# Weight decoding: more rooms for raw words, one operation moved to GpSimd and one to VectorE, a later subtraction

## The chip, the cores and the metric

The kernel runs on one core of a Trainium2 chip. A core has a matrix engine (TensorE, PE in the profile; its weight loads are PEld), three engines for elementwise work (VectorE, DVE; ScalarE, ACT; GpSimd, POOL) and SyncE (SP), whose queue issues nearly all DMA transfers here. Every engine runs its own list of instructions in order and waits on semaphores for the others. The metric is the time of one execution on the device, in microseconds (us); less is better.

## The reference

Attention with a band and a few global keys, followed by a dense MLP. There are 4 batches of 8 heads, 768 positions, head size 64; each position attends to the 8 global keys and to the 96 positions up to its own, with a linear bias by distance. The heads side by side give 3072 rows of 512, which the MLP takes through weights 512x2048 and 2048x512.

```python
def _attn_ref(q, k, v, n_global, n_local):
    scores = scale * np.matmul(q, k.transpose(0, 1, 3, 2))
    ...
    scores = np.where(keep, scores + bias, -1e9)
    a = np.exp(scores - np.max(scores, axis=-1, keepdims=True))
    return np.matmul(a / (a.sum(-1, keepdims=True) + 1e-9), v)

def _moe_ref(x, w_in, w_out):
    h = x @ w_in
    g = h * np.clip(h + 3.0, 0.0, 6.0) / 6.0
    return g @ w_out
```

q, k, v are fp32; the weights are float64, so the kernel gets each of them as two 32-bit words.

## The kernel before

The 3072 rows are 8 blocks of 384 (a batch and half of its positions). For each block four pairs of heads are attended to, and then the MLP runs over 16 columns of 128 of the hidden width. One such step f is a group of 12 matmuls (`first`, L166: four slices of 128 of the input, and three products each, high x high, low x high, high x low, since every fp32 value is split into a rounded high part and the rest), a gate (ScalarE L177, VectorE L178), the gate's own split into `gh` (a rounded copy) and `gl` (L191, VectorE), and 9 matmuls (`second`, L198). The second group waits for `gl`.

**Stages.** First the attention of blocks 0 to 2, 12 pairs, runs as a pipeline written out in `banded` (L529 to L576): scores on TensorE, weighing on VectorE (L831), exponentials on ScalarE (L835), division by the row sums on GpSimd (`normalize`, L855), transposes back on TensorE (`turn`, L863 and L865), and the product with the values (L907). From pair 10 on, the first steps of block 0's MLP are woven in. Then the rest of block 0 runs together with block 1, alternating, so that every weight is used twice. During all of this the weights are decoded. Blocks 2 to 7 follow with their weights ready, and with the attention of the block behind them woven in.

**Decoding.** There are 32 chunks of weights (128x512 values, 512 KB of raw words each; chunk 2f holds step f's part of the first weights, chunk 2f+1 that of the second). A chunk's tile `wst` comes by DMA (`fetch`, L363). The rest turns each float64 into fp32 with integer operations on its words:

- L371 ScalarE: absolute value of the high word (into `wz`)
- L378 GpSimd (the first 12 chunks, `helped`) or L400 VectorE (the other 20): clamp of the exponent
- L401 VectorE: mask and shift left by 3
- L409 VectorE: merge with sign and top bits of the high word
- L375 GpSimd: the low word times 2^-29, rounded (`we`)
- L415 VectorE: integer add of `we` to `wz`
- L419 ScalarE: the high part (`w1h`, `w2h`), a rounded copy
- L406 VectorE: the low part (`w1l`, `w2l`), by subtraction, one chunk later

`wst`, `wz` and `we` have two buffers each. The fetch of chunk i+2 comes after the merge of chunk i, which is the last to read that chunk's `wst`.

**What sets the order.** `decode` is a generator with four steps per chunk. `work(pe, dve)` keeps two sums, the TensorE time handed out and the VectorE time handed out, and lets out decoding steps as long as VectorE's sum is behind; each `yield` says what a step counts as. `decoded_to` forces steps out before the matmuls that need a chunk. `in_order` (L613) then fixes the order of TensorE, SyncE and GpSimd as the code issued it; for VectorE and ScalarE a scheduler picks the order at build time, the earlier issued first where both could run. So on GpSimd a division stands behind whatever decoding operation was let out before it. `held` is the last instruction of the first pairs' weighing; decoding's first instruction is tied behind it.

`general` is a fallback for other sizes of the band; it does not run here.

Of the kernel before, what the change touches and what calls it, by code (L numbers as in the profile page):

```python
# [9 lines left out]
F32 = mybir.dt.float32  # L10
F32R = mybir.dt.float32r
I32 = mybir.dt.int32
U32 = mybir.dt.uint32
AF = mybir.ActivationFunctionType
ALU = mybir.AluOpType
# [3 lines left out]
DM, DF = 512, 2048  # L19
P = 128  # L20
# [5 lines left out]
NF = DF // P  # L26
# [12 lines left out]
LEAST, MOST = (float(np.uint32(e << 20).view(np.float32)) for e in (896, 1151))  # L39
# [8 lines left out]
LEAD = 6  # L48
WAKE = 9
FIRST = 6  # L50

def store(nc, pool, out, row, acc, last=False):
    for tt in range(NT):
        o = pool.tile([P, DM], F32, name="o")
        nc.scalar.mul(out=o, in_=acc[tt], mul=1.0 / 6.0)
        (nc.scalar if last and tt == NT - 1 else nc.sync).dma_start(out=out[row + tt * P: row + (tt + 1) * P, :], in_=o)


class Kernel:
# [15 lines left out]
    def decoding(self, ctx, loads, bufs, **kw):  # L75

        self.wp = self.pool("wp", loads, ctx=ctx, **kw)
        self.zp = self.pool("zp", bufs, ctx=ctx, **kw)
        self.ep = self.pool("ep", bufs, ctx=ctx, **kw)

    def weights(self):

# [279 lines left out]
        self.raw[i] = self.wp.tile([P, 2 * DM], I32, name="wst")  # L362
        self.nc.sync.dma_start(out=self.raw[i], in_=self.w[i])  # L363

    def magnitude(self, i):


        words = self.raw[i].rearrange("p (c w) -> p c w", w=2)
        self.z[i] = self.zp.tile([P, DM], I32, name="wz")
        self.e[i] = self.ep.tile([P, DM], I32, name="we")  # L370
        self.nc.scalar.activation(out=self.z[i].bitcast(F32), in_=words[:, :, 1].bitcast(F32), func=AF.Abs)  # L371
        if i == 0:
            self.tc.add_manual_dep(self.nc.cur_bb.bb.instructions[-1], self.held, mybir.DependencyInfo(
                mybir.DependencyClass.NoSync, mybir.DependencyReason.DATA), reason="behind the first pairs")
        self.nc.gpsimd.tensor_scalar(out=self.e[i], in0=words[:, :, 0].bitcast(U32), scalar1=2.0 ** -29, scalar2=0.0, op0=ALU.mult, op1=ALU.add)  # L375
        if self.helped(i):
            z = self.z[i].bitcast(F32)
            self.nc.gpsimd.tensor_scalar(out=z, in0=z, scalar1=MOST, scalar2=LEAST, op0=ALU.min, op1=ALU.max)  # L378

    def helped(self, i):  # L380
        return i < 2 * FIRST

    def part(self, i, w1, w2):
        f = i // 2
        return (self.w1(w1, f), lambda a: a.rearrange("p (k c) -> p k c", k=NKT)) if i % 2 == 0 else (self.w2(w2, f), lambda a: a)

    def decode(self):

        nc = self.nc
        ts, stt, tt = nc.vector.tensor_scalar, nc.vector.scalar_tensor_tensor, nc.vector.tensor_tensor
        N = 2 * NF
        self.magnitude(0)
        for i in range(N + 1):
            a, b = i < N, i > 0
            if a:
                z = self.z[i]
                if not self.helped(i):
                    ts(out=z.bitcast(F32), in0=z.bitcast(F32), scalar1=LEAST, scalar2=MOST, op0=ALU.max, op1=ALU.min)  # L400
                ts(out=z, in0=z, scalar1=0x07FFFFFF, scalar2=3, op0=ALU.bitwise_and, op1=ALU.logical_shift_left)  # L401
            yield (0.34 if self.helped(i) else 0.68) * a
            if b:
                hi, sh = self.part(i - 1, self.w1h, self.w2h)
                lo, _ = self.part(i - 1, self.w1l, self.w2l)
                tt(out=lo, in0=sh(self.z.pop(i - 1).bitcast(F32)), in1=hi.bitcast(F32), op=ALU.subtract)  # L406
            yield 0.6 * b
            if a:
                stt(out=z, in0=self.raw[i].rearrange("p (c w) -> p c w", w=2)[:, :, 1], scalar=-0x40000000, in1=z,  # L409
                    op0=ALU.bitwise_and, op1=ALU.bitwise_or)  # L410
                if i + 2 < N:
                    self.fetch(i + 2)
            yield 0.6 * a
            if a:
                tt(out=z, in0=z, in1=self.e.pop(i), op=ALU.add)  # L415
                if i + 1 < N:
                    self.magnitude(i + 1)
                hi, sh = self.part(i, self.w1h, self.w2h)
                nc.scalar.copy(out=hi, in_=sh(z.bitcast(F32)))  # L419
            yield 0.69 * a  # L420

    def work(self, pe, dve):

# [5 lines left out]
    def decode_step(self):  # L429
        self.given[1] += next(self.decoding_steps)  # L430
        self.decoded += 1
        if self.decoded == 4 * (2 * NF + 1):
            self.decoded_all()

    def decoded_to(self, i):

        while self.decoded < 4 * (i + 1) + (2 if i < 2 * NF - 1 else 4):
            self.decode_step()

    def halves(self, steps, pool=False):  # L440
# [45 lines left out]
    def banded(self, flag):  # L486
# [6 lines left out]
        self.ps_x = self.pool("ps_x", 1, PSUM)  # L493
        self.turn, self.more, self.score_banks = {}, True, 1
        self.wake()
        self.raw, self.z, self.e, self.given, self.decoded = {}, {}, {}, [0.0, 0.0], 0
        self.last, self.op = None, None
        self.weights()
        with ExitStack() as early, ExitStack() as words:
            x0 = self.x_tiles(self.pool("x0", 1, ctx=early, side="right"))  # L500
            xs = [x0, self.x_tiles(), self.x_tiles()]
            self.decoding(words, 2, 2, side="right")
            self.decoding_steps = self.decode()

            def decoded_all():
# [3 lines left out]
            self.decoded_all = decoded_all  # L509
            self.fetch(0)  # L510
            self.given[1] = LEAD
            self.allowed = 4 * NF + 3
            acc = []
            with ExitStack() as ctx:
                self.room += self.rooms(self.pool("more", 1, ctx=ctx), MORE - ROOMS, ROOMS)
# [1 line left out]
                self.fetch(1)  # L517
                for n in range(ROOMS):
                    self.load(n, True)
                self.plain_distances(ctx)  # L520
                self.attending(ctx, 0, 9, 5)
                pairs = [Pair(self, n, xs[n // NPAIR], True) for n in range(EARLY)]
                todo = self.halves([(0, f, xs[0], acc) for f in range(FIRST)])

# [52 lines left out]
                for _ in todo:  # L577
                    pass
            self.weights()
            self.allowed = 4 * (2 * NF + 1)  # L580
            acc1 = [pool.tile([P, BANK], F32, name=name) for pool, name in ((self.ps_s, "sp"), (self.ps_t, "tp"), (self.ps_x, "xp"))]
            self.given[1] = max(self.given)
            todo = [(1, f, xs[1], acc1) for f in range(FIRST)]
            todo += [(i, f, xs[i], (acc, acc1)[i]) for f in range(FIRST, NF) for i in range(2)]
            for _ in self.halves(todo):
# [65 lines left out]
    def general_setup(self):  # L651
        self.constants()
        self.ps_o = self.pool("ps_o", NT, PSUM)
        self.common(1, 2)
        self.weights()
        self.weights()
        self.decoding(self.ctx, 1, 1)
        self.ap_ = self.pool("ap", 1)
        self.dp = self.pool("dp", 1)
        self.up = self.pool("up", 1)  # L660
        self.mp = self.pool("mp", NT)
        self.op = self.pool("op", 1)
        nc = self.nc
        ts, tt = nc.vector.tensor_scalar, nc.vector.tensor_tensor
        iv = self.dp.tile([P, 4], I32, name="iv")
        nc.sync.dma_start(out=iv, in_=self.bounds.broadcast_to([P, 4]))
        fv = self.dp.tile([P, 2, 2], F32, name="fv")
        nc.vector.tensor_copy(out=fv.rearrange("p a b -> p (a b)"), in_=iv)
        c = self.dp.tile([P, 2, 1], F32, name="c")
        lv = self.lv = self.dp.tile([P, 2, 1], F32, name="lv")  # L670
        ts(out=c, in0=fv[:, :, 0:1], scalar1=0.0, scalar2=None, op0=ALU.is_lt)
        tt(out=c, in0=c, in1=fv[:, :, 1:2], op=ALU.add)
        ts(out=c, in0=c, scalar1=2.0 ** 32, scalar2=None, op0=ALU.mult)
        tt(out=lv, in0=c, in1=fv[:, :, 0:1], op=ALU.add)
        self.masked = self.dp.tile([P, S], F32, name="masked")
        nc.vector.memset(self.masked, NEG)
# [84 lines left out]
class Pair:  # L761
# [61 lines left out]
    def weigh(self, t, sp, e, lo):  # L823
        nc, kk = self.nc, self.k
        for j in range(2):
            h, i = 2 * self.pr + j, 2 * t + j
            if self.plain:
                d, scale = (kk.p0 if lo else kk.p1)[:, h], PLAIN
            else:
                d, scale = (kk.d0 if lo else kk.d1), SLOPES[h]  # L830
            nc.vector.tensor_tensor_reduce(out=e[:, j, lo:W], in0=sp[j][:, lo:W], in1=d, op0=ALU.add, op1=ALU.min, scale=scale,  # L831
                                           scalar=3.0e38, accum_out=self.least[:, i:i + 1])
        for j in range(2):
            i = 2 * t + j
            nc.scalar.activation(out=e[:, j, lo:W], in_=e[:, j, lo:W], func=AF.Exp, bias=self.least[:, i:i + 1], scale=-1.0,  # L835
                                 accum_out=self.sums[:, 0, i:i + 1])
        if self.n <= 2:
            kk.held = nc.cur_bb.bb.instructions[-1].name
        self.rows.append(e)

    def sum_up(self, t=None):
# [145 lines left out]
```

## Time and profile before

| | us |
|---|---|
| median of 3 runs | 676.46 |
| lowest, highest | 675.81, 677.81 |
| span of the profiled execution, first to last instruction | 675.4 |
| TensorE busy in it | 658.0 |
| VectorE busy in it | 421.2 |
| GpSimd busy in it | 230.2 |

The profiled execution's own time is given as its span; the median of the timed runs is 1.1 us more, for what lies before the first and after the last instruction. The profile lists, for each engine, how long it was busy, and in slices or stretches of time in which share; for a group of instructions (one source line, one form) the count, the busy time and the mean duration, and what ended the idle time before them; and who waited for whom. In a list in order of time each line has the start, the duration, the engine, the source line, the operation, what it writes and reads, and in brackets how long the engine had been idle and what released it. Line numbers are those of the kernel before. Durations of operations that follow each other on one engine overlap a little.

### The profile page before, as it was taken

Reading aid. Unit: us, or ns where it says so; the run is one execution under the profiler, and the core shown is the slowest. Engines: PE = TensorE matmul, PEld = TensorE weight load, DVE = VectorE, ACT = ScalarE, POOL = GpSimd, SP = SyncE. Lnnn points to the kernel's source line nnn. Section 1 sums busy time; section 2 is a strip of 40 time slices with the busy share of each in tenths; the row PEclk is TensorE's granted clock in tenths of the full one; section 3 lists DMA queues with packets and bytes.
Section 4 is the critical chain, followed back from the end, with each engine's and each line's share of the span. In section 5 each row is a group of like instructions: output and inputs, shape, how many; then the busy total and the mean of one; then the engine's idle time right before and its main releaser. Section 6 shows DMA issues by size and latency. Waiting matters only on the chain.

```text
span 675.4 us, 11454 instructions
## 1 busy us (share of the span) xinstructions
PE 658.0 (97%) x3963; PEld 587.2 (87%) x3963; DVE 421.2 (62%) x1109; ACT 278.5 (41%) x736; POOL 230.2 (34%) x401
## 2 busy tenths in 40 slices
PE   9989599999999999999999999999999999999997
PEld 7769488888999999989998999899898999989995
DVE  6798889999324776557663777547763677422222
ACT  6898555655225433143332444143331434221111
POOL 5778642221001443324341444314531444302110
PEclk9999889999999999999999999999999999999999
DMA  8675444442003267635654266734455255610001
GB/s 290 185 249 183 168 151 154 138 144 94 1 1 113 67 167 195 167 95 139 151 148 125 93 161 175 195 94 117 129 166 152 71 154 142 141 48 2 1 1 52
DMA packets 60836, 84.73 MB, mean 125 GB/s; under 512 B 8416, under 2 KB 45536, under 8 KB 60768
## 3 DMA queue, kind: packets, MB, share of 16 engines
q1 hardware_dynamic: 60480, 83.64, 42.7%
q8 instruction: 33, 0.54, 0.3%
q14 instruction: 35, 0.29, 0.1%
q10 hardware_dynamic: 288, 0.26, 0.1%
HBM read 62.92 MB, written 20.97 MB: 124 GB/s over the span
## 4 chain that ended last, share of the span: by engine, by line
PE 79%; DVE 9%; DMA 5%; ACT 3%; POOL 2%; issue 2%; SPq 0%; POOLq 0%; ACTq 0%; DVEq 0%
PE hp L166 34%; PE acc L198 32%; DMA wst<-w 5%; PE xp L907 2%; PE sp L820 2%; PE tp L907 2%; DVE wz L409 2%; PE tp L820 2%; ACT n L835 2%; DVE wz L415 1%; POOL n L855 1%; PE xp L358 1%; DVE wz L401 1%; DVE n L831 1%; DVE gl L191 1%
## 5 line engine op out<-in xcount | busy, mean ns | idle before, releaser
L177 ACT ACTIVATE g<-hp,small 128x384 f32<-128x384 f32 x127 | 73.7, 580 | 251.6 <-PE hp L166 230.5
L166 PE MATMUL hp<-xh,w1h 128*128 128x384 f32 x512 | 174.0, 340 | 0.0
L166 PE MATMUL hp<-xh,w1l 128*128 128x384 f32 x512 | 172.7, 337 | 0.0
L166 PE MATMUL hp<-xl,w1h 128*128 128x384 f32 x512 | 171.9, 336 | 0.0
L184 POOL TENSOR_SCALAR gh<-g 128x384 fp32r<-128x384 f32 x96 | 51.8, 540 | 292.3 <-DVE g L178 261.7
L198 PE MATMUL acc<-w2h,gl 128*128 128x512 f32 x336 | 133.8, 398 | 0.2
L198 PE MATMUL acc<-w2l,gh 128*128 128x512 f32 x336 | 133.1, 396 | 0.0
L198 PE MATMUL acc<-w2h,gh 128*128 128x512 f32 x336 | 132.9, 395 | 0.0
L178 DVE SCALAR_TENSOR_TENSOR g<-g,hp 128x384 f32<-128x384 f32 x128 | 69.7, 545 | 90.1 <-ACT g L177 89.7
L191 DVE TENSOR_TENSOR gl<-g,gh 128x384 fp32r<-128x384 f32 x128 | 80.6, 630 | 53.2 <-POOL gh L184 44.9
L855 POOL TENSOR_SCALAR n<-n,sums 128x232 f32<-128x232 f32 (+1 forms) x186 | 103.1, 570 | 31.2 <-DVE sums L846 17.6
L835 ACT ACTIVATE n<-n,least 128x232 f32<-128x232 f32 (+1 forms) x192 | 89.3, 468 | 44.0 <-DVE least L831 42.0
L166 PEld LDWEIGHTS hp<-xh,w1h 128*128 128x128 f32 x512 | 96.3, 188 | 5.5 <-issue 1.5
L166 PEld LDWEIGHTS hp<-xl,w1h 128*128 128x128 f32 x512 | 96.2, 188 | 3.9
L166 PEld LDWEIGHTS hp<-xh,w1l 128*128 128x128 f32 x512 | 96.0, 188 | 0.0
L198 PEld LDWEIGHTS acc<-w2h,gl 128*128 128x128 f32 x336 | 63.4, 189 | 15.4 <-DVE gl L191 1.7
L198 PEld LDWEIGHTS acc<-w2h,gh 128*128 128x128 f32 x336 | 63.8, 190 | 10.4 <-POOL gh L184 0.3
L198 PEld LDWEIGHTS acc<-w2l,gh 128*128 128x128 f32 x336 | 63.6, 189 | 10.4
L880 DVE STREAM_TRANSPOSE blocks<-n 128x256 f32<-128x256 f32 x112 | 43.5, 424 | 30.5 <-POOL n L855 17.3
L375 POOL TENSOR_SCALAR we<-wst 128x512 int32<-128x512 uint32 x32 | 26.6, 832 | 64.6 <-DMA wst<-w 56.7
L791 POOL TENSOR_SCALAR kx<-load 64x504 fp32r<-64x504 f32 (+1 forms) x40 | 31.1, 778 | 43.9 <-PE hp L166 42.3
L831 DVE CUSTOM_DVE_ANT_0 n<-sp,d 128x232 f32<-128x232 f32 (+1 forms) x70 | 23.6, 374 | 29.6 <-PE sp L820 29.1
(111 smaller groups left out, 788.3 us busy)
## 6 DMA issues: line engine op xcount, KB each, us to landing
wst<-w SPq DMA_DIRECT2D x32, 512.0 KB, 3.5
load<-pairs SPq DMA_DIRECT2D x22, 636.0 KB, 5.2
there<-blocks SPq DMA_DIRECT2D x52, 256.0 KB, 2.6
load<-pairs SPq DMA_DIRECT2D x32, 384.0 KB, 4.2
weights<-there SPq DMA_DIRECT2D x48, 192.0 KB, 3.9
out<-o SPq DMA_DIRECT2D x23, 256.0 KB, 2.1
weights<-there SPq DMA_DIRECT2D x32, 160.0 KB, 3.2
load<-pairs SPq DMA_DIRECT2D x9, 444.0 KB, 4.2
```

Of the source, the lines that this page charges most:

```text
L166: self.nc.tensor.matmul(hp, lhsT=self.w1(w, f)[:, kt, :], rhs=a[:, kt, :], start=(n == 0), stop=(n == 3 * NKT - 1))
L177: nc.scalar.activation(out=g, in_=hp, func=AF.Relu, bias=self.three, scale=1.0)
L178: nc.vector.scalar_tensor_tensor(out=g, in0=g, scalar=6.0, in1=hp, op0=ALU.min, op1=ALU.mult)
L184: self.nc.gpsimd.tensor_scalar(out=gh, in0=g, scalar1=1.0, scalar2=0.0, op0=ALU.mult, op1=ALU.add)
L191: self.nc.vector.tensor_tensor(out=gl, in0=g, in1=gh.bitcast(F32), op=ALU.subtract)
L198: self.nc.tensor.matmul(acc[tt], lhsT=a[:, tk], rhs=self.w2(w, f), start=(f == 0 and j == 0), stop=(f == NF - 1 and j == 2))
L791: nc.gpsimd.tensor_scalar(out=part["kx"][own, c], in0=k[own, c], scalar1=1.0, scalar2=0.0, op0=ALU.mult, op1=ALU.add)
L820: nc.tensor.matmul(sp[j][:, lo:W], lhsT=q[:, t], rhs=part["kx"][:, c], start=(m == 0), stop=(m == 1))
L831: nc.vector.tensor_tensor_reduce(out=e[:, j, lo:W], in0=sp[j][:, lo:W], in1=d, op0=ALU.add, op1=ALU.min, scale=scale, scalar=3.0e38, accum ...
L835: nc.scalar.activation(out=e[:, j, lo:W], in_=e[:, j, lo:W], func=AF.Exp, bias=self.least[:, i:i + 1], scale=-1.0, accum_out=self.sums[:, ...
L855: nc.gpsimd.tensor_scalar(out=e[:, j, lo:W], in0=e[:, j, lo:W], scalar1=over, scalar2=0.0, op0=ALU.mult, op1=ALU.add)
L880: nc.vector.transpose(out=blocks[:, :, s].rearrange("p b j q -> p j b q"), in_=e[:, :, c:c + P].rearrange("p j (b q) -> p j b q", b=4))
```

## The change

- `wst` gets four buffers (`WORDS`) and the fetch that follows the merge of chunk i is that of chunk i+4. Fetches 2 and 3 are issued at the start, behind the first pairs' values.
- The integer add moves from VectorE to GpSimd, right after the merge in the code.
- VectorE clamps every chunk; GpSimd's clamp of the first 12 chunks is gone.
- The subtraction for the low part comes two chunks later instead of one (`LAG`), and `wz` gets three buffers. `we` keeps two.
- A chunk's four steps are cut elsewhere and count as 0.45, 0.45, 0.7 and 0.7 instead of 0.34 or 0.68, 0.6, 0.6 and 0.69. `decoded_to`, `allowed` and the total count follow.
- ScalarE's absolute value and GpSimd's low word of a chunk are issued at the chunk's own first step, and no longer at the last step of the chunk before it.
- `held` is set to the last VectorE instruction of the weighing in place of the last ScalarE one, and ties the first clamp instead of the first absolute value.
- `BARE` is 0, so the branch with `abs_max` is not taken.

```diff
+WORDS = 4
+LAG = 2
+BARE = 0
...
-        self.zp = self.pool("zp", bufs, ctx=ctx, **kw)
-        self.ep = self.pool("ep", bufs, ctx=ctx, **kw)
+        self.zp = self.pool("zp", bufs[0], ctx=ctx, **kw)
+        self.ep = self.pool("ep", bufs[1], ctx=ctx, **kw)
...
-    def magnitude(self, i):
...
-        self.nc.scalar.activation(out=self.z[i].bitcast(F32), in_=words[:, :, 1].bitcast(F32), func=AF.Abs)
...
-        self.nc.gpsimd.tensor_scalar(out=self.e[i], in0=words[:, :, 0].bitcast(U32), scalar1=2.0 ** -29, scalar2=0.0, op0=ALU.mult, op1=ALU.add)
-        if self.helped(i):
-            z = self.z[i].bitcast(F32)
-            self.nc.gpsimd.tensor_scalar(out=z, in0=z, scalar1=MOST, scalar2=LEAST, op0=ALU.min, op1=ALU.max)
...
-        self.magnitude(0)
-        for i in range(N + 1):
-            a, b = i < N, i > 0
+        for i in range(N + LAG):
+            a, b = i < N, i >= LAG
             if a:
-                z = self.z[i]
-                if not self.helped(i):
-                    ts(out=z.bitcast(F32), in0=z.bitcast(F32), scalar1=LEAST, scalar2=MOST, op0=ALU.max, op1=ALU.min)
+                words = self.raw[i].rearrange("p (c w) -> p c w", w=2)
+                low, high = words[:, :, 0], words[:, :, 1]
+                z = self.z[i] = self.zp.tile([P, DM], I32, name="wz")
+                e = self.ep.tile([P, DM], I32, name="we")
+                zf = z.bitcast(F32)
+                if i < BARE:
+                    ts(out=zf, in0=high.bitcast(F32), scalar1=LEAST, scalar2=MOST, op0=ALU.abs_max, op1=ALU.min)
+                else:
+                    nc.scalar.activation(out=zf, in_=high.bitcast(F32), func=AF.Abs)
+                    ts(out=zf, in0=zf, scalar1=LEAST, scalar2=MOST, op0=ALU.max, op1=ALU.min)
...
+                nc.gpsimd.tensor_scalar(out=e, in0=low.bitcast(U32), scalar1=2.0 ** -29, scalar2=0.0, op0=ALU.mult, op1=ALU.add)
+            yield 0.45 * a
+            if a:
                 ts(out=z, in0=z, scalar1=0x07FFFFFF, scalar2=3, op0=ALU.bitwise_and, op1=ALU.logical_shift_left)
-            yield (0.34 if self.helped(i) else 0.68) * a
-            if b:
-                hi, sh = self.part(i - 1, self.w1h, self.w2h)
-                lo, _ = self.part(i - 1, self.w1l, self.w2l)
-                tt(out=lo, in0=sh(self.z.pop(i - 1).bitcast(F32)), in1=hi.bitcast(F32), op=ALU.subtract)
-            yield 0.6 * b
+            yield 0.45 * a
             if a:
-                stt(out=z, in0=self.raw[i].rearrange("p (c w) -> p c w", w=2)[:, :, 1], scalar=-0x40000000, in1=z,
-                    op0=ALU.bitwise_and, op1=ALU.bitwise_or)
-                if i + 2 < N:
-                    self.fetch(i + 2)
-            yield 0.6 * a
-            if a:
-                tt(out=z, in0=z, in1=self.e.pop(i), op=ALU.add)
-                if i + 1 < N:
-                    self.magnitude(i + 1)
+                stt(out=z, in0=high, scalar=-0x40000000, in1=z, op0=ALU.bitwise_and, op1=ALU.bitwise_or)
+                nc.gpsimd.tensor_tensor(out=z, in0=z, in1=e, op=ALU.add)
+                if i + WORDS < N:
+                    self.fetch(i + WORDS)
                 hi, sh = self.part(i, self.w1h, self.w2h)
                 nc.scalar.copy(out=hi, in_=sh(z.bitcast(F32)))
-            yield 0.69 * a
+            yield 0.7 * a
+            if b:
+                hi, sh = self.part(i - LAG, self.w1h, self.w2h)
+                lo, _ = self.part(i - LAG, self.w1l, self.w2l)
+                tt(out=lo, in0=sh(self.z.pop(i - LAG).bitcast(F32)), in1=hi.bitcast(F32), op=ALU.subtract)
+            yield 0.7 * b
...
-        while self.decoded < 4 * (i + 1) + (2 if i < 2 * NF - 1 else 4):
+        while self.decoded < 4 * (i + LAG + 1):
...
+                for i in range(2, WORDS):
+                    self.fetch(i)
...
+        if self.n <= 2:
+            kk.held = nc.cur_bb.bb.instructions[-1].name
         for j in range(2):
             i = 2 * t + j
             nc.scalar.activation(out=e[:, j, lo:W], in_=e[:, j, lo:W], func=AF.Exp, bias=self.least[:, i:i + 1], scale=-1.0,
                                  accum_out=self.sums[:, 0, i:i + 1])
-        if self.n <= 2:
-            kk.held = nc.cur_bb.bb.instructions[-1].name
```

More of the change, by code (lines that the diff above doesn't have):

```diff
@@ L363, in fetch @@
         self.nc.sync.dma_start(out=self.raw[i], in_=self.w[i])
-    def magnitude(self, i):
[L368 to L375, printed above, removed]
-        if self.helped(i):
-            z = self.z[i].bitcast(F32)
-            self.nc.gpsimd.tensor_scalar(out=z, in0=z, scalar1=MOST, scalar2=LEAST, op0=ALU.min, op1=ALU.max)
-    def helped(self, i):
-        return i < 2 * FIRST
     def part(self, i, w1, w2):
@@ new lines, in decode @@
+                if i == 0:
+                    self.tc.add_manual_dep(nc.cur_bb.bb.instructions[-1], self.held, mybir.DependencyInfo(
+                        mybir.DependencyClass.NoSync, mybir.DependencyReason.DATA), reason="behind the first pairs")
+                nc.gpsimd.tensor_scalar(out=e, in0=low.bitcast(U32), scalar1=2.0 ** -29, scalar2=0.0, op0=ALU.mult, op1=ALU.add)
+            yield 0.45 * a
+            if a:
+                ts(out=z, in0=z, scalar1=0x07FFFFFF, scalar2=3, op0=ALU.bitwise_and, op1=ALU.logical_shift_left)
@@ L431, in decode_step @@
         self.decoded += 1
-        if self.decoded == 4 * (2 * NF + 1):
+        if self.decoded == 4 * (2 * NF + LAG):
             self.decoded_all()
     def decoded_to(self, i):
-        while self.decoded < 4 * (i + 1) + (2 if i < 2 * NF - 1 else 4):
+        while self.decoded < 4 * (i + LAG + 1):
             self.decode_step()
@@ L495, in banded @@
         self.wake()
-        self.raw, self.z, self.e, self.given, self.decoded = {}, {}, {}, [0.0, 0.0], 0
+        self.raw, self.z, self.given, self.decoded = {}, {}, [0.0, 0.0], 0
         self.last, self.op = None, None
@@ L501, in banded @@
             xs = [x0, self.x_tiles(), self.x_tiles()]
-            self.decoding(words, 2, 2, side="right")
+            self.decoding(words, WORDS, (LAG + 1, 2), side="right")
             self.decoding_steps = self.decode()
@@ L511, in banded @@
             self.given[1] = LEAD
-            self.allowed = 4 * NF + 3
+            self.allowed = 4 * NF + 2
             acc = []
@@ L579, in banded @@
             self.weights()
-            self.allowed = 4 * (2 * NF + 1)
+            self.allowed = 4 * (2 * NF + LAG)
             acc1 = [pool.tile([P, BANK], F32, name=name) for pool, name in ((self.ps_s, "sp"), (self.ps_t, "tp"), (self.ps_x, "xp"))]
@@ L656, in general_setup @@
         self.weights()
-        self.decoding(self.ctx, 1, 1)
+        self.decoding(self.ctx, 1, (1, 1))
         self.ap_ = self.pool("ap", 1)
```

## The prediction

> **What bounds the kernel now.** I read the page's parts 1 and 2 first, then busy time by stretch, then the waits of the stretch that the change touches, then GpSimd and TensorE in order of time.
>
> ```profile
> span 675.4 us, 11454 instructions
> PE 658.0 (97%) x3963; PEld 587.2 (87%) x3963; DVE 421.2 (62%) x1109; ACT 278.5 (41%) x736; POOL 230.2 (34%) x401
> PE   9989599999999999999999999999999999999997
> DVE  6798889999324776557663777547763677422222
> PEclk9999889999999999999999999999999999999999
> ```
>
> The second line says that TensorE is the bound: idle for 17.4 us of 675.4. The slices say where something can be won: PE has a 5 in the fifth slice, and the granted clock dips there. DVE is at 9 in slices 5 to 9, which is decoding, and not later. The busy times by stretch (us in each; PE, PEld, DVE, ACT, POOL; then clock and DMA) put numbers on it.
>
> ```profile
> 30.00:50.00 20.00, 16.68 (x172) 12.75 (x172) 19.47 (x76) 18.25 (x62) 14.60 (x25) 1.00 0.79 247
> 50.00:70.00 20.00, 20.00 (x151) 18.06 (x148) 16.96 (x51) 16.54 (x51) 16.63 (x25) 1.00 0.60 199
> 70.00:90.00 20.00, 12.86 (x84) 9.95 (x83) 14.87 (x24) 9.71 (x19) 13.41 (x18) 0.74 0.39 127
> 90.00:160.00 70.00, 69.07 (x356) 60.69 (x355) 68.21 (x127) 40.67 (x72) 16.84 (x19) 1.00 0.46 150
> 30.00:160.00 130.00, 118.62 (x754) 101.44 (x753) 119.51 (x275) 85.18 (x202) 61.48 (x84) 0.96 0.52 169
> ```
>
> TensorE is idle for 130 - 118.62 = 11.4 us here: 3.3 in 30 to 50, 7.1 in 70 to 90, 0.9 after. VectorE is busy for 119.5 of the same 130, so it is nearly a second bound: whatever TensorE wins has to fit VectorE's work too. VectorE's 10.5 us of idle time are 0.5, 3.0, 5.1 and 1.8. The 7.1 us are one stall. First the waits of this stretch (who waited for whom; us, times, longest), then GpSimd and TensorE in time.
>
> ```profile
> POOL we L375 <- DMA wst<-w: 56.7, 21, 4.9
> PEld tp L863 <- POOL n L855: 9.7, 5, 7.2
> ```
>
> ```profile
> 66.47 4.60 POOL L855 TENSOR_SCALAR n<-n,sums 128x128 f32<-128x128 f32 x6
> ...
> 73.56 0.67 POOL L375 TENSOR_SCALAR we<-wst 128x512 int32<-128x512 uint32 x1 [0.70 <-DMA wst<-w]
> 74.31 0.94 POOL L378 TENSOR_SCALAR wz<-wz 128x512 f32<-128x512 f32 x1
> 80.18 0.64 POOL L375 TENSOR_SCALAR we<-wst 128x512 int32<-128x512 uint32 x1 [4.93 <-DMA wst<-w]
> 80.90 0.61 POOL L378 TENSOR_SCALAR wz<-wz 128x512 f32<-128x512 f32 x1
> 81.50 4.81 POOL L855 TENSOR_SCALAR n<-n,sums 128x128 f32<-128x128 f32 x6
> ```
>
> ```profile
> 75.53 0.33 PE L166 MATMUL hp<-xh,w1l 128*128 128x384 f32 x1
> 82.74 0.99 PE L863 MATMUL tp<-ident,n 128*128 128x128 f32 x2 [6.87 <-POOL n L855]
> 83.38 0.78 PE L198 MATMUL acc<-w2h,gh 128*128 128x512 f32 x1
> ...
> 87.37 0.41 PE L863 MATMUL tp<-ident,n 128*128 128x128 f32 x1
> ```
>
> GpSimd keeps the order of the code. The division of the last pair's rows (L855, 81.50) stands behind the low words of chunk 9 (L375, 80.18), which wait 4.93 us for their load: two rooms only, and the load is issued when VectorE has merged chunk 7. TensorE's transpose of those rows is 6.87 us late, and its next nine matmuls run at the low clock: 87.37 - 83.38 = 3.99 us. At full clock nine take 2.08:
>
> ```profile
> 167.55 2.08 PE acc L198 x9
> ```
>
> So 1.9 us more. The stall is worth 6.9 + 1.9 = 8.8 us, and all that could be won here is 11.4 + 1.9 = 13.3.
>
> **The change, part by part.** The groups of the decode (busy us, mean ns | idle before):
>
> ```profile
> L415 DVE CUSTOM_DVE_ANT_0 wz<-wz,we 128x1024 uint16<-128x1024 uint16 x32 | 25.3, 791 | 0.5
> L409 DVE SCALAR_TENSOR_TENSOR wz<-wst,wz 128x512 int32<-128x512 int32 x32 | 23.7, 740 | 0.1
> L401 DVE TENSOR_SCALAR wz<-wz 128x512 int32<-128x512 int32 x32 | 13.7, 429 | 2.8 <-POOL wz L378 2.6
> L378 POOL TENSOR_SCALAR wz<-wz 128x512 f32<-128x512 f32 x12 | 9.9, 823 | 1.0
> L406 DVE TENSOR_TENSOR w2l<-wz,w2h 128x512 fp32r<-128x512 f32 x16 | 11.1, 694 | 1.6 <-ACT w2h L419 1.6
> L400 DVE TENSOR_SCALAR wz<-wz 128x512 f32<-128x512 f32 x20 | 9.7, 484 | 0.9 <-ACT wz L371 0.7
> ```
>
> 1. *Rooms and loads.* Fetch i+4 is issued where fetch i+2 was, so a chunk has two more chunk times. SP passes the same 32 fetches and waits on the same merges (L409). The wait of 4.93 us goes, and division 11 now has low words 8 and add 8 ahead of it, not chunk 9. GpSimd without DMA waits: division 10 ended at 71.1 (66.47 + 4.60), then two chunks of about 2 us each (L375's 0.67, the add's 1.0 of point 3, some waiting), so division 11 could start near 75 to 76, where TensorE arrives (75.9). I take the stall of 8.8 as gone; what is late next is VectorE. New is 1 MB more ahead of pair loads at the start, where DMA is full:
>
> ```profile
> 4.00:14.00 10.00, 9.94 (x70) 7.82 (x68) 8.08 (x53) 6.62 (x28) 5.11 (x15) 1.00 1.00 367
> ```
>
> 1.05 MB / 367 GB/s = 2.9 us is the most that a later pair's load slips; the cover is the pairs already loaded. I take 0, with 2.9 as the other end. That chunk 0's magnitude (L371) is no longer held back on ScalarE I take at 0 too, the same work earlier; at worst it delays an exponential of the first pairs by its own 0.68:
>
> ```profile
> L371 ACT ACTIVATE wz<-wst 128x512 f32<-128x512 f32 x32 | 21.6, 677 | 30.2 <-DMA wst<-w 27.4 <-DVE w1l L406 1.6 <-DVE w2l L406 1.2
> ```
>
> 2. *The add leaves VectorE, the clamp comes back.* VectorE loses 32 x 0.791 = 25.3 us and gains 12 x 0.484 = 5.8: 19.5 less in all. In 30 to 160 it decoded some 30 chunks; after it, by the accounting in `work`, a step of the MLP (4.2 given, 0.94 taken by the gate) lets out 3.26/2.3 = 1.42 chunks where 3.26/2.57 = 1.27 came before, and all 32 are out by that point. So VectorE's need in the stretch is 119.5 - 30 x 0.791 + 5.8 + 2 x 2.34 = 106.3 us, before any new interference (2.34 = 0.484 + 0.429 + 0.740 + 0.69 is a chunk's four operations).
>
> 3. *The add on GpSimd, and what it does to VectorE.* No two-input GpSimd operation of this size is in the trace. The nearest rows are VectorE's in 100 to 158, where GpSimd runs only L375 (means), and the same lines' shortest, middle and longest:
>
> ```profile
> L415 DVE CUSTOM_DVE_ANT_0 wz<-wz,we 128x1024 uint16<-128x1024 uint16 x16 | 12.8, 798 | 0.4
> L191 DVE TENSOR_TENSOR gl<-g,gh 128x384 fp32r<-128x384 f32 x13 | 8.5, 653 | 0.0
> L400 DVE TENSOR_SCALAR wz<-wz 128x512 f32<-128x512 f32 x16 | 7.9, 497 | 0.2
> ```
>
> ```profile
> L415 DVE CUSTOM_DVE_ANT_0 wz<-wz,we x16: 678/690/1137, 100.5 to 155.1; 128x1024 uint16<-128x1024 uint16 x16
> L191 DVE TENSOR_TENSOR gl<-g,gh x13: 543/547/1011, 101.4 to 152.9; 128x384 fp32r<-128x384 f32 x13
> L400 DVE TENSOR_SCALAR wz<-wz x16: 411/415/779, 101.1 to 155.9; 128x512 f32<-128x512 f32 x16
> L375 POOL TENSOR_SCALAR we<-wst x16: 661/910/1142, 99.9 to 155.3; 128x512 int32<-128x512 uint32 x16
> ```
>
> VectorE's operations are either at their shortest or about 0.4 longer, and so is L375: the two hold each other up. Mean above shortest: 16 x 0.120 + 13 x 0.110 + 16 x 0.086 = 4.7 us, so one L375 of 0.66 us alone costs VectorE 0.29 us on average; a full hit costs 1.137 - 0.678 = 0.46, its length less 0.2. The add reads two inputs: its length lies between 0.66 (as L375) and 1.32 (twice that); I take 1.0. Its cost to VectorE, x, scaled with length: 0.29 x 1.0/0.66 = 0.44. Ends: 0 (always beside an operation that reads PSUM) and 1.32 - 0.2 = 1.1 (always a full hit at the longest).
>
> [...]
>
> 4. *Last subtraction two chunks later* costs VectorE nothing: the same 32 operations, with more time for GpSimd's add and ScalarE's rounding ahead of them. Chunks are still out before each "need" of the first and second matmuls: by the accounting chunk 16 is let out at block 1's second step and first needed twelve steps later, which is the cover; without it TensorE would wait for a whole chunk, 2.34 us and more.
>
> **The sum.** VectorE's need is 106.3 + 32x; of its idle time the 5.1 us in 70 to 90 go and 5.4 stay. Change of the stretch: 106.3 + 32 x 0.44 + 5.4 - 130 = -4.2 us. So TensorE wins 8.8 at the stall and pays back about 4.6, a little in every step to 160, waiting for `gl` (L191). After the decode TensorE sets the pace as before. The profiled span is 675.4, the median of the runs 676.46; I set the change on the median: **672.2 us**.
>
> **Rivals.**
> - *Every add is a full hit (slower).* The add is released when the merge (L409) ends, and VectorE's next operations are mostly of the kind that collides. For it: the pattern 678 or 1137 above. Against: 4.7 us are only ten full hits' worth among 16 L375. Price 1.0 - 0.2 = 0.8: 106.3 + 25.6 + 5.4 - 130 = +7.3, 683.8 us. It decides from x = 0.57, where the sum is zero. It keeps VectorE busy without gaps in 90 to 160, with `gl` late in each step.
> - *A new wait takes the old one's place (no change).* GpSimd is in order, so division 11 waits behind an add that waits for VectorE's merge. GpSimd was busy for 31.2 of 40 us in 30 to 70 already. If 4 of the 8.8 us stay, the sum is -0.2: 676.3.
> - *Adds cheap, VectorE clear of the bound.* x at 0.2: 106.3 + 6.4 + 5.4 - 130 = -11.9, near the ceiling of 13.3: 664.6.
> - *The loads do not come earlier*, since a fetch still waits in SP's order behind pair loads: then the 4.93 us stay, and it is the second rival.
>
> **Chances.** A difference of 0.3% (2 us) is what a measurement of this kernel can tell from none. Forecast 0.36 (669.5 to 674.4); cheap adds 0.14; no change 0.20; full hits 0.30. So faster 0.50, same 0.20, slower 0.30. The range reaches from the cheap adds (664) to just over the full hits (685).
>
> **What would show it.** Right: no DMA wait before L375's successor; TensorE's clock at 1.00 in 70 to 90 and less than 1 us idle at the last transposes; the GpSimd add near 1.0 us; the decode's VectorE operations longer by 0.3 to 0.5 us per add. Wrong: an add over 1.2 us, TensorE idle by several us in 90 to 160 behind `gl`, or division 11 late behind an add.

## The result, and the profile after

| | before | after |
|---|---|---|
| median, us | 676.51 (4 runs) | 706.75 (4 runs) |
| lowest, highest | 675.81, 677.81 | 705.71, 707.54 |
| span of the profiled execution | 675.4 | 703.8 |

The ratio is 1.0444, with a 95% interval of 1.0428 to 1.046: slower by 30 us. The forecast was 672.2, the range ended at 685, and the rival on that side stood at 683.8. The mechanism of that rival is there, but it explains only part of the time.

The page of the kernel after, the same lines as before the change:

```profile
span 703.8 us, 11413 instructions
PE 665.7 (95%) x3963; PEld 592.4 (84%) x3963; DVE 432.1 (61%) x1089; ACT 277.6 (39%) x736; POOL 262.9 (37%) x421
PE   8978777778999999999999999999999999999997
DVE  6898899995222467655665387636665477522222
PEclk9999997899999999999999999999999999999999
```

VectorE was to be busy for some 5 us less (32 adds gone, clamps back, adds felt); it is busy for 10.9 us more, with 20 instructions fewer. TensorE idles for 38.1 us instead of 17.4. The 5 in the fifth slice is gone; in its place PE is at 7 in six of the first nine slices. By stretch (us busy in each: PE, PEld, DVE, ACT, POOL; then clock and DMA):

```profile
30.00:50.00 20.00, 15.74 (x152) 12.81 (x154) 17.43 (x63) 18.41 (x61) 15.48 (x26) 0.91 0.67 205
50.00:70.00 20.00, 18.48 (x157) 16.01 (x153) 17.81 (x54) 15.86 (x49) 18.01 (x24) 1.00 0.67 228
70.00:90.00 20.00, 15.29 (x111) 12.64 (x110) 17.10 (x35) 12.96 (x31) 16.39 (x19) 1.00 0.51 171
90.00:160.00 70.00, 52.19 (x224) 42.70 (x222) 70.00 (x94) 32.41 (x59) 42.70 (x38) 0.88 0.39 134
30.00:160.00 130.00, 101.71 (x636) 84.17 (x636) 122.34 (x243) 79.64 (x197) 92.57 (x105) 0.92 0.50 165
```

From 70 to 90 TensorE has won 2.4 us (12.86 to 15.29). From 90 to 160, where it was idle for 0.9 us, it is idle for 17.8, at a granted clock of 0.88, and VectorE is busy for 70.00 of 70. So VectorE sets the pace there. The waits of 90 to 160 name the path by which TensorE feels it (who waited for whom; us, times, longest):

```profile
PEld sp L201 <- DVE gl L194: 12.5, 6, 2.8
PE sp L201 <- DVE gl L194: 9.9, 6, 2.3
```

Before, the first of these was 2.1 us. What VectorE does there, grouped from 95 to 155 us; first the kernel before, then the kernel after (count | busy us, mean ns | idle before):

```profile
L415 DVE CUSTOM_DVE_ANT_0 wz<-wz,we 128x1024 uint16<-128x1024 uint16 x16 | 13.2, 826 | 0.3
L409 DVE SCALAR_TENSOR_TENSOR wz<-wst,wz 128x512 int32<-128x512 int32 x17 | 11.6, 681 | 0.0
L191 DVE TENSOR_TENSOR gl<-g,gh 128x384 fp32r<-128x384 f32 x14 | 9.0, 645 | 0.0
```

```profile
L411 DVE TENSOR_TENSOR w1l<-wz,w1h 128x512 fp32r<-128x512 f32 x8 | 14.2, 1771 | 0.0
L411 DVE TENSOR_TENSOR w2l<-wz,w2h 128x512 fp32r<-128x512 f32 x8 | 14.1, 1768 | 0.0
L401 DVE SCALAR_TENSOR_TENSOR wz<-wst,wz 128x512 int32<-128x512 int32 x16 | 10.9, 681 | 0.0
L398 DVE TENSOR_SCALAR wz<-wz 128x512 int32<-128x512 int32 x17 | 9.4, 551 | 0.0
L391 DVE TENSOR_SCALAR wz<-wz 128x512 f32<-128x512 f32 x16 | 6.7, 416 | 0.0
L194 DVE TENSOR_TENSOR gl<-g,gh 128x384 fp32r<-128x384 f32 x8 | 6.6, 828 | 0.0
```

Two things are to be seen. **One:** the subtraction (L411) takes 1.77 us where it took 0.68. A chunk now costs VectorE 1.77 + 0.68 + 0.55 + 0.42 = 3.42 us; it was to be 2.78. **Two:** in 60 us the kernel before merged 17 chunks and made 14 `gl`, one for each step of the MLP; the kernel after merged 16 chunks and made 8. Decoding runs at the same rate in time, but takes 2.0 chunks a step instead of 1.2. Six steps fewer at 60/14 = 4.3 us are 26 of the 30 us.

The first of the two in order of time, GpSimd and then VectorE:

```profile
119.65 1.30 POOL L402 TENSOR_TENSOR wz<-wz,we 128x512 int32<-128x512 int32 x1 [1.86 <-DVE wz L401]
122.75 1.30 POOL L402 TENSOR_TENSOR wz<-wz,we 128x512 int32<-128x512 int32 x1 [0.72 <-ACT w2h L406]
```

```profile
118.80 0.68 DVE L401 SCALAR_TENSOR_TENSOR wz<-wst,wz 128x512 int32<-128x512 int32 x1
119.40 0.41 DVE L398 TENSOR_SCALAR wz<-wz 128x512 int32<-128x512 int32 x1
119.74 1.76 DVE L411 TENSOR_TENSOR w1l<-wz,w1h 128x512 fp32r<-128x512 f32 x1
121.42 0.54 DVE L181 SCALAR_TENSOR_TENSOR g<-g,hp 128x384 f32<-128x384 f32 x1
```

The merge ends and releases GpSimd's add, which starts at 119.65. VectorE's next operation but one, the subtraction, starts 0.09 us later and ends at 121.50: the add's end (120.95) and 0.55 more, a little less than the 0.68 it needs by itself. Nearly every add of this stretch meets a subtraction so. The profile names ScalarE as the releaser of some, but all 19 adds from 95 to 165 start 0.85 to 0.87 us after their merge has started, and 18 of them 0.07 to 0.09 us ahead of a subtraction. By line in the same stretch (shortest/middle/longest, ns):

```profile
L402 POOL TENSOR_TENSOR wz<-wz,we x19: 1287/1300/1577, 96.7 to 164.4; 128x512 int32<-128x512 int32 x19
L411 DVE TENSOR_TENSOR w1l<-wz,w1h x10: 685/1772/1783, 96.8 to 164.1; 128x512 fp32r<-128x512 f32 x10
L411 DVE TENSOR_TENSOR w2l<-wz,w2h x9: 1754/1764/1780, 99.9 to 160.5; 128x512 fp32r<-128x512 f32 x9
L181 DVE SCALAR_TENSOR_TENSOR g<-g,hp x10: 539/541/548, 98.5 to 164.7; 128x384 f32<-128x384 f32 x10
```

18 of 19 subtractions take some 1.08 us more than the 0.68 they need. One is at its shortest: it started 0.26 us ahead of its add, and there the add is the longer one, 1.58 instead of 1.30. The gate's multiply L181, which reads one operand from PSUM, is never held up (539 to 548 ns); in the kernel before, from 100 to 158, the same multiply took 538 to 550 ns, and L375 ran beside five of its 14 from start to end. The excess of the 18 is the add's 1.30 less 0.2.

This holds once the decoding runs steadily. Before 95 us the subtractions are hardly hit (12 of them from 28 us on, 0.69 in the middle and 1.15 at the longest); the mean of all 32 is 1.31 us. There other operations can be hit, as a clamp at 93.30 that takes 1.52 us, where the later ones (L391) take 0.42. Over the whole run the 32 adds cost VectorE 432.1 - (421.2 - 25.3 + 5.8) = 30.4 us net, or 0.95 each.

### The profile page after: what moved, and what is told of

Same layout as the page of the kernel before. It is cut to its first block, busy times and chain, and to the rows that moved or that the text cites. A ratio compares the mean times of both kernels' runs of the same rounds, so it can differ in the third digit from the quotient of the medians.

```text
span 703.8 us, 11413 instructions
## 1 busy us (share of the span) xinstructions
PE 665.7 (95%) x3963; PEld 592.4 (84%) x3963; DVE 432.1 (61%) x1089; ACT 277.6 (39%) x736; POOL 262.9 (37%) x421
## 4 chain that ended last, share of the span: by engine, by line
PE 80%; DVE 11%; issue 3%; POOL 3%; ACT 2%; DMA 1%; SPq 0%; POOLq 0%; DVEq 0%; ACTq 0%
PE hp L169 34%; PE acc L201 31%; PE xp L901 3%; PE sp L814 2%; DVE w1l L411 2%; PE tp L901 2%; DVE wz L398 2%; PE tp L814 2%; DVE wz L401 2%; DVE w2l L411 1%; POOL n L849 1%; DVE wz L391 1%; POOL wz L402 1%; ACT n L831 1%; DVE gl L194 1%
## 5 line engine op out<-in xcount | busy, mean ns | idle before, releaser
L181 DVE SCALAR_TENSOR_TENSOR g<-g,hp 128x384 f32<-128x384 f32 x128 | 69.7, 545 | 108.4 <-ACT g L180 108.1
L849 POOL TENSOR_SCALAR n<-n,sums 128x232 f32<-128x232 f32 (+1 forms) x186 | 100.1, 553 | 34.7 <-DVE sums L840 18.9
L169 PEld LDWEIGHTS hp<-xh,w1h 128*128 128x128 f32 x512 | 97.8, 191 | 5.7 <-issue 1.5
L402 POOL TENSOR_TENSOR wz<-wz,we 128x512 int32<-128x512 int32 x32 | 43.8, 1369 | 29.1 <-DVE wz L401 18.4
```

Of the source, the lines that this page charges most:

```text
L169: self.nc.tensor.matmul(hp, lhsT=self.w1(w, f)[:, kt, :], rhs=a[:, kt, :], start=(n == 0), stop=(n == 3 * NKT - 1))
L181: nc.vector.scalar_tensor_tensor(out=g, in0=g, scalar=6.0, in1=hp, op0=ALU.min, op1=ALU.mult)
L402: nc.gpsimd.tensor_tensor(out=z, in0=z, in1=e, op=ALU.add)
L849: nc.gpsimd.tensor_scalar(out=e[:, j, lo:W], in0=e[:, j, lo:W], scalar1=over, scalar2=0.0, op0=ALU.mult, op1=ALU.add)
```

## The experiments

Each edit is to the kernel after unless it says otherwise. Ratios are to the kernel before, which ran beside each (676.57 to 676.84 us in its four sets of runs), with 95% intervals.

### One part at a time

**e1: the add back on VectorE**, all else as after.

```diff
-                nc.gpsimd.tensor_tensor(out=z, in0=z, in1=e, op=ALU.add)
+                tt(out=z, in0=z, in1=e, op=ALU.add)
```

> The changed kernel with the integer add back on VectorE, all else as changed (four rooms, VectorE clamps, subtraction two chunks later). Theory A, the price: each GpSimd add of 1.3 us holds VectorE's next operation for about 1.08 us, 32 x 1.08 = 34.6 us. Without it VectorE pays 32 x 0.6 for the add itself, so the decode's VectorE work falls by about 15 us and the time to about 690 at most, with the subtraction back at 0.68 us. Theory B, the order: VectorE's list, made at build time, holds two chunks per MLP step where before it held 1.2, so the gates of TensorE's steps come late whatever a chunk costs. The list of this kernel holds 1.5 chunks per step, at about 2.8 us a chunk and 0.94 for the gate: 5.1 us per step against TensorE's 4.2 over some 13 steps, 12 us lost, near 680. Both together say 676 to 685; above 695 A falls.

Measured: 683.91 us, 1.012 (1.0087 to 1.0154).

**e2: no add at all** (the line left out; the weights lack their lowest bits).

> The changed kernel without the integer add (the low words are rounded and not used, so the weights lack their last bits); all else as changed. Theory A (price of the add): nothing holds VectorE but the low words' operation, a chunk costs it 1.88 + 0.3 = 2.2 us, and the stall at the last transposes is gone too: 664 to 668. Theory B (order): the list still holds 1.85 chunks per step, 1.85 x 2.2 + 0.94 = 5.0 us per step against 4.2 over 15 steps: 12 us lost and 9 to 11 won, 676 to 680.

Measured: 679.43 us, 1.0039 (1.0025 to 1.0053).

**e3: only the four rooms**, put into the kernel before.

```diff
+WORDS = 4
...
-                if i + 2 < N:
-                    self.fetch(i + 2)
+                if i + WORDS < N:
+                    self.fetch(i + WORDS)
...
-            self.decoding(words, 2, 2, side="right")
+            self.decoding(words, WORDS, 2, side="right")
...
+                for i in range(2, WORDS):
+                    self.fetch(i)
```

> The kernel before with four rooms for raw words and the fetch of chunk i+4, nothing else of the change. If the stall of 6.9 us at the last transposes and the low clock after it come from the late load, and loads are all that rooms change, 8.8 us go: about 668. If the rooms themselves are the harm (they let VectorE's list run ahead, theory B in its plain form), it is slower than 680. Its list holds one chunk per step in most steps, as before, so B as the list shows it says 668 too.

Measured: 671.07 us, 0.9916 (0.9891 to 0.9942). TensorE's waits at the last transposes in e3, which were 6.87 us:

```profile
78.47 0.33 PE L866 MATMUL tp<-ident,n 128*128 128x128 f32 x1 [1.98 <-POOL n L858]
79.65 0.47 PE L866 MATMUL tp<-ident,n 128*128 128x128 f32 x1 [0.85 <-POOL n L858]
```

What follows: the rooms win 5.6 us. The add on GpSimd costs 706.75 - 683.91 = 22.8 us. e1 lies where price and order together put it, and e2 where the order puts it (676 to 680), not where the price alone does (664 to 668). For e1 is still 12.8 us slower than e3, from which it differs in the clamps, the counting, the order of issue and the lag; and even without any add (e2) VectorE's relief of 32 additions leaves the kernel slower than before. Something in that rest costs more than 10 us. Two stretches of e2 show where it goes:

```profile
110.00:130.00 20.00, 16.59 (x80) 13.82 (x79) 20.00 (x37) 12.76 (x22) 5.00 (x7) 1.00 0.55 181
150.00:160.00 10.00, 10.00 (x51) 9.00 (x50) 2.73 (x5) 2.77 (x5) 0.00 (x0) 1.00 0.01 2
```

From 110 to 130 VectorE is busy all the time and TensorE is idle for 3.4 us; from 150 to 160 VectorE has little to do. The decoding is over early (from 150 to 160 VectorE is busy for 2.73 of 10 us, in e3 for 9.86), and TensorE has waited for it.

### The lag, or the order that comes with it

VectorE's order is made when the kernel is built. With three `wz` buffers and a subtraction that may come two chunks later, more decoding operations can run before a gate, and where they were issued earlier they are put first. Two runs take the lag back to one.

**f1: LAG = 1, add on VectorE** and **f2: LAG = 1, add on GpSimd.**

```diff
-LAG = 2
+LAG = 1
...
-                nc.gpsimd.tensor_tensor(out=z, in0=z, in1=e, op=ALU.add)
+                tt(out=z, in0=z, in1=e, op=ALU.add)
```

(the last two lines in f1 alone)

> The changed kernel with the add on VectorE and the subtraction one chunk later instead of two (so two buffers of wz). VectorE's list then holds one chunk per MLP step in most steps, like that of the kernel with four rooms only. Order theory: what the kernel with the add on VectorE lost against four rooms only (683.9 against 671.1) came from the list of 1.5 chunks per step, so this one gives most of it back: 671 to 676, the upper end for the 12 clamps of 0.48 us that VectorE has more. Rival: it came from the clamps and the other counting, and this one stays at 681 to 685.

> The changed kernel, add on GpSimd, with the subtraction one chunk later instead of two. VectorE's list holds 1.3 chunks per step in place of 2. Order and price together: 1.3 x 3.3 + 0.94 = 5.2 us per step against 4.2 over some 15 steps, 15 us lost where 33 were: 686 to 692. Price alone (32 adds cost the same wherever they stand): 703 to 707.

Measured: f1 671.01 us, 0.9933 (0.9908 to 0.9957); f2 689.98 us, 1.0194 (1.017 to 1.0218). So the four cells are:

| us | lag 2 | lag 1 | lag costs |
|---|---|---|---|
| add on GpSimd | 706.75 | 689.98 | 16.8 |
| add on VectorE | 683.91 | 671.01 | 12.9 |
| the add's place costs | 22.8 | 19.0 | |

The merges and the `gl` of 95 to 155 us tell why; first e1 (lag 2), then f1 (lag 1):

```profile
L401 DVE SCALAR_TENSOR_TENSOR wz<-wst,wz 128x512 int32<-128x512 int32 x17 | 11.6, 680 | 0.0
L194 DVE TENSOR_TENSOR gl<-g,gh 128x384 fp32r<-128x384 f32 x11 | 6.0, 547 | 0.0
```

```profile
L194 DVE TENSOR_TENSOR gl<-g,gh 128x384 fp32r<-128x384 f32 x15 | 12.4, 826 | 0.0
L401 DVE SCALAR_TENSOR_TENSOR wz<-wst,wz 128x512 int32<-128x512 int32 x16 | 10.9, 679 | 0.0
```

17 chunks beside 11 steps with lag 2, 16 beside 15 with lag 1. Four steps of 60/15 = 4.0 us are 16 us; 12.9 were measured. TensorE's weight loads waited for `gl` (into `sp`, 90 to 160 us) for 9.5 us in e1 and 0.9 in f1. But a lag of one also takes a buffer away and brings each subtraction forward, so these two runs don't yet say that it is the order.

**e4: VectorE tied to the order of the code** in `in_order`, as TensorE and GpSimd are, with a chunk counted as 2.6 instead of 2.3.

```diff
-            if i.engine in (mybir.EngineType.PE, mybir.EngineType.SP, mybir.EngineType.Pool) and "Tile" not in type(i).__name__:
+            if i.engine in (mybir.EngineType.PE, mybir.EngineType.SP, mybir.EngineType.Pool, mybir.EngineType.DVE) and "Tile" not in type(i).__name__:
```

> The changed kernel, add on GpSimd, with VectorE's order tied to the order of the code and a chunk's steps counted as 2.6 instead of 2.3, so that its list holds 1.25 chunks per MLP step in place of 2. The adds are the same 32. Theory A alone (the price counts, not the place): about 706, as changed. Theory B (VectorE's work per step decides): 1.25 x 3.3 + 0.94 = 5.1 us per step against 7.6 measured; over 16 steps 14 us are lost to TensorE's 4.2 where some 33 were: 685 to 690.

Measured: 776.45 us, 1.1481 (1.1451 to 1.1511), far from both. Its stretch of 30 to 160, and waits of 28 to 220:

```profile
30.00:160.00 130.00, 97.12 (x595) 81.79 (x590) 78.68 (x196) 64.73 (x166) 62.45 (x83) 0.87 0.39 127
```

```profile
DVE g L181 <- ACT g L180: 30.7, 8, 5.5
PEld hp L169 <- DVE w1l L411: 27.1, 6, 5.6
```

VectorE is busy for only 78.68 of 130 us: in its fixed order it stands still for what isn't ready yet (30.7 us for the gate's first half from ScalarE), and TensorE's next step waits for weights (27.1). That is another kernel, and it decides nothing between the two theories.

**f8 and f9: a light tie.** Each chunk's clamp is tied behind the last `gl` issued before it, and a chunk counts as 2.6. Lag, buffers and operations stay. f8 has the add on GpSimd, f9 on VectorE.

```diff
+        self.gated = self.nc.cur_bb.bb.instructions[-1].name
...
+                    if i > 0 and self.gated is not None:
+                        self.tc.add_manual_dep(nc.cur_bb.bb.instructions[-1], self.gated, mybir.DependencyInfo(
+                            mybir.DependencyClass.NoSync, mybir.DependencyReason.DATA), reason="behind the step")
...
-            yield 0.45 * a
+            yield 0.5 * a
...
-            yield 0.7 * a
+            yield 0.8 * a
```

> The changed kernel, add on GpSimd, two chunks' lag, with one tie more: a chunk's clamp stands behind the last gl issued before it in the code, and a chunk counts as 2.6, so that VectorE's list cannot run ahead of TensorE's steps. It holds 1.25 chunks per step. Nothing else is tied, unlike in the kernel with VectorE's whole order fixed. Order theory: 1.25 x 3.3 + 0.94 = 5.1 us per step against 7.6 measured in the changed kernel, over 16 steps 14 us lost: 685 to 690. Price alone: 703 to 707.

> The kernel after with the add on VectorE (683.9 us; 671.0 with a lag of one) and, as in f8, each chunk's clamp tied behind the last gl already built and 2.6 given for a chunk. Lag of two, three z rooms and all operations stay; only VectorE's order changes, to some 1.25 chunks between two gates. If the cost of the lag is the order (chunks ahead of the gates): 671 to 677 us. Rival (the lag or the third room costs by itself, whatever the order): 682 to 686.

Measured: f8 693.97 us, 1.0253 (1.0231 to 1.0276); f9 669.4 us, 0.9896 (0.9864 to 0.9928). In f9 from 95 to 155, and its stretch from 90 to 160:

```profile
L405 DVE SCALAR_TENSOR_TENSOR wz<-wst,wz 128x512 int32<-128x512 int32 x17 | 11.5, 680 | 0.0
L194 DVE TENSOR_TENSOR gl<-g,gh 128x384 fp32r<-128x384 f32 x15 | 8.7, 578 | 0.0
```

```profile
90.00:160.00 70.00, 69.35 (x340) 60.60 (x338) 69.86 (x132) 40.37 (x70) 18.86 (x19) 1.00 0.40 129
```

What follows: with the lag of two and all three `wz` buffers, order and counting alone take e1 from 683.9 to 669.4, and the kernel after from 706.75 to 693.97. f9 decodes 17 chunks beside 15 steps, and TensorE is busy for 69.35 of 70 us. So the lag and the third buffer by themselves cost nothing that f9 shows, and the order that they allowed does. Which of the two, the tie or the counting, did more, these runs don't say. f9 came out just under its 671 to 677. f8 missed its 685 to 690 by 4 us: the tie took 12.8 us off, fewer than expected.

### The price of the add

**f6: a one-input operation in the add's place**, a multiplication by one in place (the low words are not added).

```diff
-                nc.gpsimd.tensor_tensor(out=z, in0=z, in1=e, op=ALU.add)
+                nc.gpsimd.tensor_scalar(out=zf, in0=zf, scalar1=1.0, scalar2=0.0, op0=ALU.mult, op1=ALU.add)
```

> The changed kernel with GpSimd's add replaced by an operation of the same size and place with one input (multiply by one, in place; the low words are not added). VectorE's list still holds 2 chunks per step. If GpSimd holds VectorE's next operation for its own length less 0.2 us, a one-input operation of 0.64 us holds it for 0.45 in place of 1.08: 32 x 0.63 = 20 us less, near 687. If the hold does not follow the length (a fixed cost, or one that only two inputs have), either 704 or more, or near the 679.4 of the kernel without any add.

Measured: 689.07 us, 1.0185 (1.0158 to 1.0212), near the 687 expected. The operation and a subtraction, 95 to 165 us:

```profile
L402 POOL TENSOR_SCALAR wz<-wz x18: 622/684/931, 95.6 to 149.1; 128x512 f32<-128x512 f32 x18
L411 DVE TENSOR_TENSOR w1l<-wz,w1h x9: 677/680/1148, 98.0 to 146.9; 128x512 fp32r<-128x512 f32 x9
```

At the same place in GpSimd's list, nothing (e2) gives 679.4, 0.68 us give 689.1 and 1.30 us give 706.75: 9.6 and 27.3 us more, or 0.30 and 0.85 for each of the 32. The longest subtraction is 0.47 us over its 0.68 in f6 and 1.10 in after, 0.2 less than the 0.68 and the 1.30; in f6 the middle one isn't hit, and which GpSimd operation the longest one met is not shown (the subtraction of 1.14 us at 124.65 met a low word of 0.76). The three kernels also differ in VectorE's order, so the 0.30 and 0.85 hold that too.

**f4: the kernel before with one line changed**, the add on GpSimd (two rooms, lag of one, clamps as before).

> The kernel before (two rooms, last subtraction one chunk later, clamps shared) with one line changed: the add on GpSimd. It prices the add without the other parts. Theory: each add of 1.30 us holds up the VectorE operation beside it by 1.08 us where VectorE's own add cost 0.79, so VectorE needs 32 x 0.29 = 9.3 us more; in the kernel after with a lag of one the same edit cost 19.0 us. Expected 686 to 696 us. Rival 1 (the add costs so much only beside four rooms and the clamps on VectorE): 676 to 682. Rival 2 (VectorE gains what it is relieved of, as I predicted): under 676.

Measured: 695.18 us, 1.0266 (1.0249 to 1.0284): 18.3 us, inside the range. But not by the reason given. Its stretch of 30 to 160, waits of 28 to 220, and its clamp from 110 to 168:

```profile
30.00:160.00 130.00, 108.58 (x681) 91.39 (x680) 98.88 (x223) 77.63 (x187) 85.67 (x105) 0.92 0.48 152
```

```profile
POOL wz L415 <- DVE wz L409: 28.6, 14, 4.5
PEld tp L863 <- POOL n L855: 14.2, 5, 8.6
DVE w1l L406 <- ACT w1h L419: 10.0, 4, 6.6
```

```profile
L400 DVE TENSOR_SCALAR wz<-wz x14: 422/820/1514, 110.8 to 164.3; 128x512 f32<-128x512 f32 x14
```

With a lag of one it is the next chunk's clamp that is held up. But VectorE is busy for 98.88 us instead of 119.51: it is not short of time, it waits. The add makes a chunk's chain longer (merge, add, ScalarE's copy, subtraction), and the divisions on GpSimd come later (TensorE's transposes wait 14.2 us for them instead of 9.7). How the other 14 of the 18.3 us divide between the chain and the held-up operations, these runs don't say.

### Towards a faster kernel

**f3: the kernel before with four rooms and all clamps on VectorE; g1: with four rooms and GpSimd clamping 8 chunks instead of 12.**

```diff
-        return i < 2 * FIRST
+        return i < 8
```

(g1; `return False` in f3; the rooms as in e3)

> The kernel before with four rooms and all 32 clamps on VectorE (12 of them were on GpSimd); the add stays on VectorE, one chunk of lag. Theory: four rooms alone gave 671.1 us with 2.8 us of TensorE's wait left at the last transposes, for a division on GpSimd that stands behind clamps; without clamps on GpSimd it starts earlier, while VectorE does 12 x 0.48 = 5.8 us more: expected 669 to 673. Rival (VectorE is the bound of 30 to 160 as soon as it gets 5.8 us more): 674 to 678.

> The kernel before with four rooms, and GpSimd clamping the first 8 chunks only instead of 12. Theory: chunks 8 and on are the ones whose clamps stand ahead of the last division on GpSimd; VectorE does 4 x 0.48 = 1.9 us more. Expected 668 to 671 us. Rival (the division waits for low words and ScalarE's magnitude as before): 671 to 673.

Measured: f3 670.67 us, 0.9913 (0.9897 to 0.993); g1 666.38 us, 0.9849 (0.9833 to 0.9865), the fastest of all, and faster than expected; f3 is inside its 669 to 673. The last transposes in g1:

```profile
76.07 0.68 PE L866 MATMUL tp<-ident,n 128*128 128x128 f32 x2 [0.16 <-POOL n L858]
```

The wait of 6.87 us is 0.16, and the clock granted from 30 to 160 is 1.00. In e3, GpSimd's list in time shows what had stood ahead of the last division, the clamp of chunk 9, which waits for ScalarE:

```profile
77.31 0.75 POOL L379 TENSOR_SCALAR wz<-wz 128x512 f32<-128x512 f32 x1 [1.93 <-ACT wz L372]
78.05 4.31 POOL L858 TENSOR_SCALAR n<-n,sums 128x128 f32<-128x128 f32 x6
```

In g1 that division starts at 74.81, and the kernel is 10.5 us faster than before. Taking all clamps off GpSimd, as f3 does, is not better: from 30 to 160 TensorE is busy for 121.61 us in f3 and for 125.80 in g1.

## Why the prediction was wrong, point by point

1. **Rooms and loads: the mechanism was right, the size short.** The load's wait is gone and the stall shrinks. The term was 8.8 us; the rooms alone gave 5.6, since the division then waits for clamps and ScalarE's magnitude (2.8 us are left). g1, in which the stall is gone, won 10.5 us (four clamps fewer on GpSimd may be a part of it), so the term was about what was there to be won. The prediction named this wait as a rival, but saw adds ahead of the division, not clamps. In the kernel after itself the load's wait is gone too, but the last division starts at 79.44 instead of 75 to 76, 2.13 us of it waiting for ScalarE. The extra early loads cost half a microsecond at most: over the first 30 us TensorE is busy for 28.49 us in e3 and 29.02 before.
2. **The ledger of VectorE: its chunks per step were wrong.** It took 1.42 chunks a step from the accounting in `work`. The kernel after has 2.0, and the kernel before, which the same accounting put at 1.27, has 1.2. The accounting says when operations are issued, not where the scheduler puts them.
3. **The add on GpSimd: mis-sized twice.** Its length was taken as 1.0 us and measured 1.30, at the upper bound given (1.32). With the add on VectorE the kernels are 18 to 25 us faster (before against f4, f1 against f2, e1 against after, f9 against f8). And x was taken as 0.44, an average over chance meetings. Once the decoding runs steadily, the meeting is not chance: the merge releases the add, and a two-input subtraction follows on VectorE 0.26 us after it (the merge at 118.80). x was 1.08 from 95 us on, the upper bound again, and 0.95 over all 32 adds. The rival "every add is a full hit" had the mechanism and the sign, but took the length of 1.0.
4. **The later subtraction "costs VectorE nothing": this step failed.** It costs nothing as work, and 12.9 to 16.8 us through the order: with two chunks ahead of each gate, `gl` is late by their length, and TensorE has nothing else to do.

The prediction's own sum with x = 0.95 is 106.3 + 30.4 + 5.4 - 130 = +12.1, or 688.6; with 1.08 for every add it is +16.3, or 692.8. With the lag taken back, f2 measured 689.98. That the sum comes so near is in part luck: it counts on 8.8 us at the stall, where the rooms alone gave 5.6, and on 5.4 us of idle time of VectorE in 30 to 160, where f2 has 12.1. The 16.8 us between f2 and the kernel after are step 4. So of the miss of 34.6 us, 16 to 21 are a price that lay within its bounds and was set near the middle, and the other 14 to 18 an effect that wasn't in the sum at all. Of the result, 676.5 to 706.75, the runs make: rooms -5.6, order +12.8 (shown by f1 and f9, which bring e1 back to 671.0 and 669.4), the add's place +22.8. The clamps back on VectorE, the new counting and the new places of issue together cost nothing that can be measured (f1 671.01, e3 671.07).

Why did more chunks a step cost time in e1, where VectorE does just as much work in all? Because while weights are decoded VectorE needs as long as TensorE. At 1.1 to 1.2 chunks a step both need 4.0 to 4.3 us (f1, f9 and before), and neither waits much. At 1.5 or 2.0 VectorE needs longer in every step, 60/11 = 5.5 us in e1 and 60/8 = 7.5 in the kernel after, TensorE falls behind, and as TensorE is the bound from there on, what it lost is not made up when the decoding ends. e2 shows both halves of it: TensorE idle while VectorE is full, and VectorE idle afterwards.

What stays open: why the tie in f8 regained 12.8 us and not the 16.8 of the lag (VectorE waits there: from 90 to 160 it is busy for 59.41 us of 70), and how the cost of the add divides in the kernels with a lag of one.

## What to carry to other kernels

When an operation moves to GpSimd, look at what releases it and which VectorE operation comes next: here a fixed order brought the two together, they met nearly every time (18 of 19 once the decoding ran steadily), and the price was 1.08 us of the add's 1.30 and not a mean over chance meetings. A further buffer and a later consumer were not free where a scheduler orders VectorE (12.9 and 16.8 us): count, in the trace, how much of the side work stands between two steps of the main chain. And try the parts singly: the one part tried here that won, with the clamps behind it out of the last division's way, gave 666.4 us.

## What the runs showed of the hardware that was not expected

GpSimd's two-input add of 128x512 int32 took 1.30 us (the middle of 19, after), and its one-input operations of that size 0.62 (f6) and 0.64 (L375 before) at the shortest and 0.68 in the middle of f6, about half. VectorE's held-up operation was longer by the GpSimd operation less 0.2 us, at both lengths (before, L415 at 122.30 took 1.13 in place of 0.68 beside an L375 of 0.66; after, 1.08 to 1.10 more beside the add of 1.30). Where the subtraction started first, the add was the longer one (1.58). In f4 a clamp with a single input was held up as well, to 1.51 us at the longest from 0.42, while the gate's multiply with an operand in PSUM never was (536 to 555 ns); whether PSUM is the reason, no run shows.
